# Reordering the start of a fused attention and feed-forward kernel: earlier third pair, later weight conversion, identity products

## The chip, the cores and the metric

The kernel runs on one core of a Trainium2 chip. The metric is the device time of one execution in microseconds (us), median over several executions. Engines are abbreviated as in the profile: PE is TensorE's matmuls, PEld its weight loads, DVE is VectorE, ACT ScalarE, POOL GpSimd, SP SyncE; SPq is SyncE issuing DMAs.

## The reference

Eight sequences of 448 tokens, 12 heads of 64: attention with normalised queries and keys, then a SwiGLU feed-forward layer over 3584 tokens.

```python
q_n, k_n = rmsnorm(q, g_q), rmsnorm(k, g_k)              # q, k, v: (8, 12, 448, 64) f32
scores = (1 / sqrt(64)) * q_n @ k_n^T
attn = softmax(scores); attn_out = attn @ v
x = attn_out.transpose(0, 2, 1, 3).reshape(3584, 768)
xn = rmsnorm(x, rms_g)
out = (silu(xn @ w_gate) * (xn @ w_val)) @ w_out          # 768x1536, 768x1536, 1536x768, held in f64
```

## The kernel before

The program is one hand-made schedule. It works on pairs of heads ("pair" `g`, 48 in all) and issues the steps of several pairs interleaved; the instructions of each engine stand in its stream in the order of issue. The steps of a pair (PSUM is the memory into which PE writes here, in banks):

```python
def load_pair(g):   # SP: q of both heads in one DMA, k in two
def squares(g, i):  # ACT squares q (i=0) or k (i=1); one PE step later DVE sums them,
                    # then POOL makes 1/rms and, for q, the normalised qn
def turn(g, i):     # PE transposes qn (i=0) or k (i=1); ACT (q) or DVE (k) evicts to qkT
def score(g, cs):   # PE: two key blocks for two heads = 4 products into 4 PSUM banks;
                    # ACT: 4 exponentials (row factor of k as scale)
def values(g):      # PE: exp(scores) x v
def sums(g):        # PE: denominators, "den"; DVE: reciprocal and product
```

The weights come as 64-bit floats and are converted meanwhile. One call of `convert()` is one turn of a pipeline over 72 pieces of 384 KB:

```python
def convert():                       # shortened
    n = turn_of["n"]; turn_of["n"] += 1
    # piece n-4: POOL adds the two halves
    # piece n-3: DVE joins (3 instructions)
    # piece n-2: ACT splits (2 instructions: `top`, `raw`)
    # piece n:   SP loads it (DMA `raw<-in_moe_w_...`)
    # piece n-6: SP stores the converted block (`kept<-w`)
```

The beginning, with cuts:

```python
    for g in range(2):
        load_pair(g)
    ...                                  # constants
    for g in range(2):
        load_v(g)
    ...                                  # three small loads: rg, row, row
    squares(0, 0)
    pe(idle)
    squares(0, 1)
    pe(lambda: turn(0, 1))
    convert(); convert(); bound()
    squares(1, 0); squares(1, 1)
    pe(lambda: turn(0, 0))
    convert()
    for g in range(NG + 1):
        load_pair(g + 2)
        if g <= NPAIR:
            pe(lambda: score(g, (0, 1)))
            squares(g + 2, 0); squares(g + 2, 1)
            if g == 0:
                pe(lambda: score(g, (2, 3)))
            convert()
            pe(lambda: turn(g + 1, 0)); pe(lambda: turn(g + 1, 1))
            if g:
                pe(lambda: values(g - 1))
            load_v(g + 2)
            convert()
            if g:
                pe(lambda: sums(g - 1))
                pe(lambda: score(g, (2, 3)))
            convert()
            continue
        ...
```

Of the kernel before, what the change touches and what calls it, by code (L numbers as in the profile page):

```python
# [8 lines left out]
F32 = mybir.dt.float32  # L9
# [325 lines left out]
def safe_scores(  # L335
# [20 lines left out]
    nc = tc.nc  # L356

    def pool(name, bufs, **kw):
        return ctx.enter_context(tc.tile_pool(name=name, bufs=bufs, **kw))

    NW, NH = 27, 14
    const, small = pool("c_const", 1), pool("c_small", 4)
# [5 lines left out]
    ps_s, ps_m, ps_f = pool("c_ps_s", 4, space=PSUM), pool("c_ps_m", 1, space=PSUM), pool("c_ps_f", 3, space=PSUM)  # L368
# [9 lines left out]
    def after(n, fn):  # L378
        due.append((now["t"] + n, fn))

    def pe(fn):
        now["t"] += 1
        fn()
        for item in [d for d in due if d[0] <= now["t"]]:
            due.remove(item)
            item[1]()
# [4 lines left out]
    def load_pair(g):  # L391
        if g >= NG:
            return
        b, hp = divmod(g, NPAIR)
        hs = slice(2 * hp, 2 * hp + 2)
        qk = st["qk", g] = qk_pool.tile([P, 2, 2 * NT * D], F32, name="qk")
        nc.sync.dma_start(out=qk[:, 0].rearrange("p (h n) -> p h n", h=2), in_=q[b, hs].rearrange("h (p t) d -> p h (t d)", t=NT))

        for h in range(2):
            nc.sync.dma_start(out=qk[:, 1].rearrange("p (t h d) -> p h t d", h=2, d=D)[:, h],  # L400
                              in_=k[b, 2 * hp + h].rearrange("(p t) d -> p t d", t=NT))

    def load_v(g):
        if g >= NG:
            return
        b, hp = divmod(g, NPAIR)
        vt = st["v", g] = v_pool.tile([P, 2, NT, D], F32, name="vt")
        nc.sync.dma_start(out=vt.rearrange("p h t d -> p h (t d)"),
                          in_=v[b, 2 * hp:2 * hp + 2].rearrange("h (p t) d -> p h (t d)", t=NT))
# [5 lines left out]
    def squares(g, i):  # L415

        if g >= NG:
            return
        n = 2 * NT
        if i == 0:  # L420
            st["ms", g] = small.tile([P, 2 * n], F32, name="ms")
        ms = st["ms", g]
        sq = tmp.tile([P, n * D], F32, name="sq", tag="sq", bufs=2)
        nc.scalar.activation(sq, st["qk", g][:, i], ACT.Square)  # L424

        def reduce():
            nc.vector.tensor_reduce(out=ms[:, i * n:(i + 1) * n], in_=sq.rearrange("p (n d) -> p n d", d=D), axis=AX_X, op=ALU.add)  # L427

        after(1, reduce)
        if g <= 1:  # L430

            after(1, lambda: rms_qk(g, slice(i * n, (i + 1) * n)))
            if i == 0:
                after(1, lambda: norm_q(g))
        elif i == 1:
            after(2, lambda: rms_qk(g))
            after(2, lambda: norm_q(g))
# [14 lines left out]
    def turn(g, i):  # L452

        if g >= NG:
            return
        if ("qkT", g) not in st:
            st["qkT", g] = qkT_pool.tile([128, 2, S], F32, name="qkT")
        src = st.pop(("qn", g)) if i == 0 else st["qk", g][:, 1]
        ps = (ps_m if todo else ps_f).tile([128, 512], F32, name="tr", tag="m" if todo else "f")
        for t in range(NT):  # L460
            nc.tensor.transpose(ps[:, t * P:(t + 1) * P], src[:, t * 2 * D:(t + 1) * 2 * D], ident[0:P, 0:P])  # L461
        dst, flat = st["qkT", g][:, i, :], ps[:, 0:S]
        if i == 0:
            nc.scalar.activation(dst, flat, ACT.Copy, scale=gqk[:, 0:1])  # L464
        else:
            nc.vector.tensor_copy(dst, flat)
# [28 lines left out]
    def values(g):  # L495

        vt = st["v", g]
        av = st["av", g] = ps_m.tile([128, 512], F32, name="av", tag="m")
        for c in range(NT):
            for j in range(2):  # L500
                nc.tensor.matmul(av[j * D:(j + 1) * D, 0:S], lhsT=vt[:, j, c, :], rhs=st["e", g, c, j],  # L501
                                 start=(c == 0), stop=(c == NT - 1))
# [113 lines left out]
    def room(n):  # L616
        return len(free_w) + max(len(free_h) - 4, 0) >= n
# [5 lines left out]
    def data(key):  # L623
        return st[key][0][:, 0:BW]
# [47 lines left out]
    def convert():  # L672

        n = turn_of["n"]
        if n >= TURNS or not room(1):
            return False
        turn_of["n"] += 1
        if 0 <= n - 4 < len(pieces):
            key = pieces[n - 4][0]
            st[key] = block()  # L680
            lo, top = st.pop(("cv", n - 4))
            nc.gpsimd.tensor_tensor(data(key).bitcast(I32), top, lo, ALU.add)  # L682
        if 0 <= n - 3 < len(pieces):
            st["cv", n - 3] = join(*st.pop(("cv", n - 3)))
        if 0 <= n - 2 < len(pieces):
            st["cv", n - 2] = split(st.pop(("raw", n - 2)))
        if n < len(pieces):
            st["raw", n] = load_raw(pieces[n][1])
        if 0 <= n - 6 < len(pieces):
            keep(pieces[n - 6][0])  # L690
        if turn_of["n"] == TURNS:

            free_w.extend(cv_pool.tile([128, BW], F32, name="top") for _ in range(4))
        return True
# [398 lines left out]
    ident = const.tile([128, 128], F32, name="ident")  # L1093
# [9 lines left out]
    for a in range(2):  # L1103
        rows = slice(a * D, (a + 1) * D)
        nc.scalar.dma_start(out=gq[rows, :], in_=g_q.rearrange("(p o) -> p o", o=1))
        nc.scalar.dma_start(out=gk[rows, :], in_=g_k.rearrange("(p o) -> p o", o=1))
    for g in range(2):
        load_v(g)
    rg = const.tile([128, NDC], F32, name="rg")
    nc.sync.dma_start(out=rg, in_=moe_rms_g.rearrange("(c p) -> p c", p=128))  # L1110
    row = const.tile([1, 2, D], F32, name="row")
    nc.sync.dma_start(out=row[:, 0, :], in_=g_q.rearrange("(o d) -> o d", o=1))
    nc.sync.dma_start(out=row[:, 1, :], in_=g_k.rearrange("(o d) -> o d", o=1))
    gqk = const.tile([128, 1], F32, name="gqk")

    def bound():
        nc.vector.scalar_tensor_tensor(gqk, gq, 1.0 / D**0.5, gk, ALU.mult, ALU.mult)

        nc.vector.tensor_scalar(gqk, gqk, SAFE / D, -SAFE / D, ALU.min, ALU.max)
        nc.vector.tensor_tensor(row[:, 0, :], row[:, 0, :], row[:, 1, :], ALU.mult)  # L1120
        top = const.tile([1, 1], F32, name="top")
        nc.vector.tensor_reduce(out=top, in_=row[:, 0, :], axis=AX_X, op=ALU.max, apply_absolute_value=True)
        nc.vector.tensor_scalar(flag, top, 8.0, SAFE, ALU.mult, ALU.is_gt)


    squares(0, 0)
    pe(idle)
    squares(0, 1)
    pe(lambda: turn(0, 1))
    convert()  # L1130
    convert()
    bound()
    squares(1, 0)
    squares(1, 1)
    pe(lambda: turn(0, 0))
    convert()
    for g in range(NG + 1):
        b, hp = divmod(g, NPAIR)
        load_pair(g + 2)
        if g <= NPAIR:  # L1140
            pe(lambda: score(g, (0, 1)))
            squares(g + 2, 0)
            squares(g + 2, 1)
            if g == 0:
                pe(lambda: score(g, (2, 3)))
            convert()
            pe(lambda: turn(g + 1, 0))
            pe(lambda: turn(g + 1, 1))
            if g:
                pe(lambda: values(g - 1))  # L1150
            load_v(g + 2)
            convert()
            if g:
                pe(lambda: sums(g - 1))
                pe(lambda: score(g, (2, 3)))
            convert()
            continue

        if g < NG:
# [3 lines that stand above are left out]
        if g == NPAIR + 1:  # L1163
            pe(lambda: rms_x(0))
            pe(lambda: score(g, (2, 3)))
            pe(lambda: norm_x(0))
        pe(lambda: sums(g - 1))
        if g == NPAIR + 1:
            begin(0, 15)
        elif g < NG:  # L1170
            pe(lambda: score(g, (2, 3)))
        if hp:
            fill()
            squares(g + 2, 0)
            squares(g + 2, 1)
            pe(lambda: turn(g + 1, 0))
            fill()
            pe(lambda: turn(g + 1, 1))
            fill()
            continue  # L1180
        fill(3)
        pe(lambda: turn(g + 1, 0))
        fill(1)
        pe(lambda: rms_x(b - 1))
        squares(g + 2, 0)
        squares(g + 2, 1)
        pe(lambda: turn(g + 1, 1))
        fill(len(todo))
        begin(b - 1, 16)
        pe(lambda: norm_x(b - 1))  # L1190
        fill()
# [41 lines left out]
```

## Time and profile before

| | before |
|---|---|
| time, median of 3 runs | 1632.63 us (1631.97 to 1633.83) |
| span of the profiled execution | 1629.0 us |
| PE busy | 1607.8 us |
| granted clock below full | 0.50 for 3.4 us, 20.2 to 23.6 us; the trace has no clock record before 13.4 us |
| second half of the second pair's scores starts | 30.40 us |

The last row is the landmark: PE does the same work up to it in both kernels (but for the added products), so its shift is the lead. Landmarks are read from the chain of work that ended last; a timeline has the same start 0.07 us earlier, because it lets matmuls overlap. PE is busy 99% of the span; a gain has to come from its few idle stretches or from the 3.4 us in which its clock is halved. The lines of the profile are in the prediction.

### The profile page before, as it was taken

The page shows a single profiled execution, that of the slowest core. Times are in us where ns is not written, and L with a number is a line of the kernel's source. Part 1 is how long each engine was busy: PE and PEld are TensorE (multiplying, and loading weights), DVE is VectorE, ACT ScalarE, POOL GpSimd, SP SyncE. Part 2 cuts the span into 40 slices and gives each one's busy share as a digit, 9 for nine tenths or more (in the row PEclk, how much of TensorE's full clock was granted, in tenths as well). Part 3 has the DMA queues.
Part 4 walks back from the last instruction along what each step waited for, and adds up shares of the span by engine and source line. Part 5 has one row for each costly group of instructions (what it writes and reads, how often), then busy time and mean ns, then how long its engine had stood idle before and what let it go on. Part 6 is the DMA issues. An engine that isn't in the chain of part 4 may idle for free.

```text
span 1629.0 us, 21534 instructions
## 1 busy us (share of the span) xinstructions
PE 1607.8 (99%) x7352; PEld 1136.8 (70%) x7352; DVE 871.8 (54%) x1425; ACT 499.9 (31%) x975; POOL 632.7 (39%) x569
## 2 busy tenths in 40 slices
PE   7999999999999999999999999999999999999998
PEld 3444445678855888568875788658886587969984
DVE  6988998377842545435562354624565234433431
ACT  7756563232322332233233222322332123100110
POOL 6778777344433434244333333334353322100000
PEclk9999999999999999999999999999999999999999
DMA  7756674576865555565544755466454463557651
GB/s 202 223 165 200 188 225 146 163 231 203 264 191 168 155 156 150 175 189 158 159 118 125 206 154 154 120 211 188 140 158 126 148 193 109 151 182 238 174 149 45
DMA packets 249036, 276.83 MB, mean 170 GB/s; under 512 B 66644, under 2 KB 245844, under 8 KB 248916
## 3 DMA queue, kind: packets, MB, share of 16 engines
q1 hardware_dynamic: 248596, 275.34, 56.6%
q8 instruction: 61, 1.00, 0.3%
q14 instruction: 59, 0.48, 0.1%
q10 hardware_dynamic: 320, 0.00, 0.0%
HBM read 235.93 MB, written 39.32 MB: 169 GB/s over the span
## 4 chain that ended last, share of the span: by engine, by line
PE 91%; DVE 5%; DMA 2%; ACT 1%; SPq 0%; issue 0%; POOL 0%; DVEq 0%; ACTq 0%; POOLq 0%
PE ff L797 40%; PE ff L991 21%; PE sc L476 9%; PE av L501 9%; PE den L512 3%; PE ff L892 3%; PE ff L1022 2%; PE tr L461 2%; DVE top L646 1%; DVE top L644 1%; DVE rd L520 1%; DVE top L645 1%; ACT e L480 1%; DMA qk<-in_k_dram 1%; DMA raw<-in_moe_w_out_dram 0%; DMA raw<-in_moe_w_gate_dram 0%
## 5 line engine op out<-in xcount | busy, mean ns | idle before, releaser
L797 PE MATMUL ff<-x,w 128*128 128x224 f32 x1728 | 352.3, 354 | 0.8 <-DVE u L809 0.8
L797 PEld LDWEIGHTS ff<-x,w 128*128 128x128 f32 x1728 | 324.1, 190 | 12.1 <-issue 8.6
L797 PE MATMUL ff<-xs,w 128*128 128x224 f32 x1326 | 272.5, 353 | 0.4 <-DVE cc L809 0.4
L480 ACT ACTIVATE e<-sc,rs 112x448 f32<-112x448 f32 x384 | 211.9, 635 | 192.1 <-PE sc L476 187.0
L486 POOL TENSOR_TENSOR es<-e 112x448 f32<-112x448 f32 x82 | 95.2, 1181 | 437.3 <-ACT e L480 437.3
L797 PEld LDWEIGHTS ff<-xs,w 128*128 128x128 f32 x1326 | 248.7, 190 | 5.4 <-issue 4.7
L490 POOL TENSOR_TENSOR es<-es,e 112x448 f32<-112x448 f32 x164 | 186.0, 1145 | 85.5 <-ACT e L480 79.1
L991 PE MATMUL ff<-w,h 128*128 128x384 f32 x594 | 202.8, 487 | 0.0
L520 DVE RECIPROCAL rd<-rd 128x448 f32<-128x448 f32 x41 | 121.0, 2952 | 137.6 <-ACT rd L519 137.6
L476 PE MATMUL sc<-qkT 64*112 64x448 f32 x768 | 179.0, 570 | 3.9 <-ACT qkT L464 3.9
L991 PEld LDWEIGHTS ff<-w,h 128*128 128x128 f32 x594 | 111.5, 190 | 76.6 <-issue 2.7
L501 PE MATMUL av<-e,vt 112*64 112x448 f32 x768 | 154.9, 545 | 0.0
L444 POOL TENSOR_TENSOR rs<-ms,mhalf 112x16 f32<-112x16 f32 (+1 forms) x50 | 143.7, 2875 | 4.2
L476 PEld LDWEIGHTS sc<-qkT 64*112 64x112 f32 x768 | 69.0, 174 | 97.0 <-issue 71.0
L991 PE MATMUL ff<-w,so 128*128 128x384 f32 x338 | 117.3, 488 | 1.4 <-DVE y L952 1.4
L501 PEld LDWEIGHTS av<-e,vt 112*64 112x64 f32 x768 | 50.8, 136 | 95.3 <-issue 74.5
L1022 PE MATMUL ff<-x,w 128*128 128x448 f32 x288 | 112.0, 542 | 0.0
L809 DVE TENSOR_TENSOR cc<-ff,u 128x448 f32<-128x448 f32 x84 | 52.3, 623 | 93.4 <-PE ff L797 93.0
L991 PEld LDWEIGHTS ff<-w,so 128*128 128x128 f32 x338 | 63.2, 190 | 45.9 <-DVE y L952 2.6
L427 DVE TENSOR_REDUCE ms<-sq 112x8 f32<-112x512 f32 x96 | 61.2, 677 | 52.6 <-ACT sq L424 52.6
L1022 PEld LDWEIGHTS ff<-x,w 128*128 128x128 f32 x288 | 53.3, 190 | 50.9 <-issue 49.0
L682 POOL TENSOR_TENSOR w<-top,raw 128x384 int32<-128x384 int32 x72 | 78.5, 1105 | 25.1 <-DVE top L646 7.3
(101 smaller groups left out, 1693.9 us busy)
## 6 DMA issues: line engine op xcount, KB each, us to landing
w<-kept SPq DMA_DIRECT2D x479, 192.0 KB, 3.2
w<-kept_o SPq DMA_DIRECT2D x294, 192.0 KB, 2.7
kept<-w SPq DMA_DIRECT2D x89, 192.0 KB, 3.7
top<-kept SPq DMA_DIRECT2D x73, 192.0 KB, 3.2
qk<-in_q_dram SPq DMA_DIRECT2D x48, 224.0 KB, 3.7
qk<-in_k_dram SPq DMA_DIRECT2D x96, 112.0 KB, 3.5
vt<-in_v_dram SPq DMA_DIRECT2D x48, 224.0 KB, 2.8
raw<-in_moe_w_gate_dram SPq DMA_DIRECT2D x24, 384.0 KB, 4.6
```

Source lines behind the costliest of these rows:

```text
L427: nc.vector.tensor_reduce(out=ms[:, i * n:(i + 1) * n], in_=sq.rearrange("p (n d) -> p n d", d=D), axis=AX_X, op=ALU.add)
L444: nc.gpsimd.tensor_tensor(st["rs", g][:, cols], ms, mhalf[0:P, cols], ALU.pow)
L476: nc.tensor.matmul(ps[0:P, 0:S], lhsT=qkT[r, 1, c * P:(c + 1) * P], rhs=qkT[r, 0, :], start=True, stop=True)
L480: nc.scalar.activation(e, ps[0:P, 0:S], ACT.Exp, scale=rs[:, n:n + 1])
L486: nc.gpsimd.tensor_tensor(es, st["e", g, 0, j], st["e", g, 1, j], ALU.add)
L490: nc.gpsimd.tensor_tensor(es, es, st["e", g, c, j], ALU.add)
L501: nc.tensor.matmul(av[j * D:(j + 1) * D, 0:S], lhsT=vt[:, j, c, :], rhs=st["e", g, c, j], start=(c == 0), stop=(c == NT - 1))
L520: nc.vector.reciprocal(rd, rd)
L682: nc.gpsimd.tensor_tensor(data(key).bitcast(I32), top, lo, ALU.add)
L797: nc.tensor.matmul(bank[:, w * HT:(w + 1) * HT], lhsT=wt[:, c * 128:(c + 1) * 128], rhs=x[:, c, :], start=onto is None and w == c == 0, st ...
L991: nc.tensor.matmul(ps, lhsT=a, rhs=data(("wo", b, name, c)), start=first and c == 0, stop=c == NFP - 1, skip_group_check=True)
L1022: nc.tensor.matmul(bank[w][:, 0:S], lhsT=data(key)[:, c * 128:(c + 1) * 128], rhs=st["x", 0, half][:, c, :], start=half == c == 0, stop=ha ...
```

## The change

The intent is to get PE to its steady work sooner. The third pair's load goes ahead of the second values and the weights; the third pair's squares go ahead of the first exponentials on ACT; the first weight conversions come later; the first values stand ahead of the third pair's transpositions on PE, to give its normalisation time; and 12 products of the identity with itself run on PE while it waits for data, to raise the clock. The diff, cut to its core:

```diff
-    for g in range(2):
-        load_v(g)
+    load_v(0)
+    load_pair(2)
+    load_v(1)
 ...                                  # the small loads go into load_rows(), two
 ...                                  # gain products out of bound() into gains()
+    def warm(n):
+        ps = ps_m.tile([128, 512], F32, name="warm", tag="m")
+        for _ in range(n):
+            nc.tensor.matmul(ps[:, 0:128], lhsT=ident, rhs=ident, start=True, stop=True)
     squares(0, 0)
+    warm(9)
     pe(idle)
     squares(0, 1)
     pe(lambda: turn(0, 1))
-    convert()
-    convert()
-    bound()
+    gains()
     squares(1, 0)
     squares(1, 1)
+    warm(3)
     pe(lambda: turn(0, 0))
-    convert()
+    squares(2, 0)
+    squares(2, 1)
     for g in range(NG + 1):
-        load_pair(g + 2)
+        if g:
+            load_pair(g + 3)
+        if g == 0:
+            pe(lambda: score(0, (0, 1)))
+            pe(lambda: score(0, (2, 3)))
+            for i in range(2):
+                pe(lambda: turn(1, i))
+            for _ in range(3):
+                convert()
+            load_pair(3)
+            load_v(2)
+            convert()
+            load_rows()
+            continue
         if g <= NPAIR:
             pe(lambda: score(g, (0, 1)))
 ...
+            if g == 1:
+                pe(lambda: values(0))
             pe(lambda: turn(g + 1, 0))
             pe(lambda: turn(g + 1, 1))
-            if g:
+            if g > 1:
                 pe(lambda: values(g - 1))
 ...
+            if g == 2:
+                bound()
             continue
```

More of the change, by code (lines that the diff above doesn't have):

```diff
@@ L1106, in safe_scores, with gains, load_rows, bound @@
         nc.scalar.dma_start(out=gk[rows, :], in_=g_k.rearrange("(p o) -> p o", o=1))
-    for g in range(2):
-        load_v(g)
+    load_v(0)
+    load_pair(2)
+    load_v(1)
+    gqk = const.tile([128, 1], F32, name="gqk")
     rg = const.tile([128, NDC], F32, name="rg")
-    nc.sync.dma_start(out=rg, in_=moe_rms_g.rearrange("(c p) -> p c", p=128))
     row = const.tile([1, 2, D], F32, name="row")
-    nc.sync.dma_start(out=row[:, 0, :], in_=g_q.rearrange("(o d) -> o d", o=1))
-    nc.sync.dma_start(out=row[:, 1, :], in_=g_k.rearrange("(o d) -> o d", o=1))
-    gqk = const.tile([128, 1], F32, name="gqk")
-    def bound():
+    def gains():
         nc.vector.scalar_tensor_tensor(gqk, gq, 1.0 / D**0.5, gk, ALU.mult, ALU.mult)
         nc.vector.tensor_scalar(gqk, gqk, SAFE / D, -SAFE / D, ALU.min, ALU.max)
+    def load_rows():
+        nc.sync.dma_start(out=rg, in_=moe_rms_g.rearrange("(c p) -> p c", p=128))
+        nc.sync.dma_start(out=row[:, 0, :], in_=g_q.rearrange("(o d) -> o d", o=1))
+        nc.sync.dma_start(out=row[:, 1, :], in_=g_k.rearrange("(o d) -> o d", o=1))
+    def bound():
         nc.vector.tensor_tensor(row[:, 0, :], row[:, 0, :], row[:, 1, :], ALU.mult)
@@ L1143, in safe_scores @@
             squares(g + 2, 1)
-            if g == 0:
-                pe(lambda: score(g, (2, 3)))
             convert()
+            if g == 1:
+                pe(lambda: values(0))
             pe(lambda: turn(g + 1, 0))
             pe(lambda: turn(g + 1, 1))
-            if g:
+            if g > 1:
                 pe(lambda: values(g - 1))
@@ L1152, in safe_scores @@
             convert()
-            if g:
-                pe(lambda: sums(g - 1))
-                pe(lambda: score(g, (2, 3)))
+            pe(lambda: sums(g - 1))
+            pe(lambda: score(g, (2, 3)))
             convert()
+            if g == 2:
+                bound()
             continue
```

## The prediction

> **What bounds the kernel now.** I read four views of the kernel before, in this order: the page, the waits of the tensor engine, its timeline at the beginning, and the chain of work that ended last. The page says that the tensor engine (PE) is busy throughout, at full clock.
>
> ```profile
> span 1629.0 us, 21534 instructions
> PE 1607.8 (99%) x7352; PEld 1136.8 (70%) x7352; DVE 871.8 (54%) x1425; ACT 499.9 (31%) x975; POOL 632.7 (39%) x569
> ...
> PE   7999999999999999999999999999999999999998
> ```
>
> Only the first slice (40.7 us) and the last are not full. PE idles 1629.0 - 1607.8 = 21.2 us in all, and its waits, longest first, place that idle time:
>
> ```profile
> PE tr L461 <- DMA qk<-in_k_dram: 4.9, 1, 4.9
> PE sc L476 <- ACT qkT L464: 3.9, 2, 3.2
> PE tr L461 <- POOL qn L448: 2.6, 1, 2.6
> PE ff L991 <- DVE y L952: 2.0, 3, 0.7
> ```
>
> The columns are the total, the number of times and the longest, in us. The first three, 4.9 + 3.9 + 2.6 = 11.4 us, all lie before 20 us: the first load, the first normalised queries, and the eviction of the second pair's transposed queries. The others sum to 3.6 us. The last 6 us are the final eviction and store. A change to the beginning can therefore act on those 11.4 us, and on what PE does slowly between them. The PE timeline of the beginning (start, duration) shows both:
>
> ```profile
> 4.95 0.98 PE L461 MATMUL tr<-ident,qk 112*128 112x112 f32 x4 [4.95 <-DMA qk<-in_k_dram]
> 8.52 1.01 PE L461 MATMUL tr<-ident,qn 112*128 112x112 f32 x4 [2.59 <-POOL qn L448]
> 10.26 5.54 PE L476 MATMUL sc<-qkT 64*112 64x448 f32 x16 [0.72 <-ACT qkT L464]
> ...
> 19.92 3.10 PE L476 MATMUL sc<-qkT 64*112 64x448 f32 x8 [3.21 <-ACT qkT L464]
> ```
>
> The last row, four score products, takes 3.10 us. The same four take 1.69 us in the chain at 95 us. From 20.2 to 23.6 us the granted clock is 0.50 in narrow windows: PE idled at 16.7 to 19.9 us[...]. The chain says what held it:
>
> ```profile
> 10.07 5.57 DMA qk<-in_k_dram
> 15.64 0.02 issue
> 15.66 0.04 ACTq L424
> 15.70 0.04 issue
> 15.74 0.63 ACT sq L424
> 16.37 2.10 ACT e L480 x4
> 18.47 0.44 ACT top L638
> 18.91 0.44 ACT raw L639
> 19.35 0.53 ACT qkT L464
> 19.88 0.04 issue
> 19.92 3.10 PE sc L476 x8
> 23.02 1.22 PE tr L461 x8
> 24.24 3.16 PE av L501 x16
> 27.40 3.01 PE den L512 x16
> 30.40 4.23 PE sc L476 x16
> ```
>
> ScalarE (ACT) stands in the middle: the squares of the third pair wait for its keys (the third pair's load is queued after three weight loads and landed at 15.64), the second four exponentials stand behind those squares, then a weight conversion, and only then the eviction PE needs. From 30.40 us on PE never idles for longer than 0.7 us.
>
> [...] Here they are full (DMA share 1.13 from 10 to 15 us, 311 GB/s)[...].
>
> **The change part by part.** I compare the order of instructions of both kernels engine by engine. PE has the same instructions in the same order but for 12 identity products and one move: the first values now stand before, not after, the third pair's transpositions. The landmark for the gain is the second half of the second pair's scores, 30.40 us before; everything on PE up to it is the same work in both.
>
> (1) First queries. Their path (load, squares, sums, power, product on GpSimd (POOL), ready at 8.46) is not touched: first transposition at 8.52. At full clock it ends about 0.45 us sooner; ACT evicts (0.63) and the first scores start at about 9.8 instead of 10.26.
>
> (2) Loads. The third pair takes the places of the second values, the 768-element gain load and two small rows: q at about 5.65 us, k at 6.2 and 6.8. v and the gain load issued at those times took 3.4 to 3.5 us. By then 448+448+224+448 KB = 1.6 MB have to arrive; the windows before had moved 1.46 MB by 9 us and 1.66 MB by 10 us. I estimate the last k at about 10.3 instead of 15.64.
>
> (3) ACT. New order: eviction (to 9.75), square of q (to 10.4), square of k (to 11.0), then eight exponentials without a break, 0.55 us each (2.19/4): 11.0 + 4.4 = 15.4. Their row factors are ready at 10.48 (POOL, 8.84 + 1.64). No conversion (0.88) stands before the eviction: 15.4 to 16.0. It needs the second pair's transposition: its qn on POOL comes at about 13.5, as the vector engine (DVE) no longer sits behind the row load until 10.19 before the next sums; PE is free for it at 13.7, when the fourth exponential has released a bank.
>
> (4) PE. Second scores start at 16.0 instead of 19.92: 3.9 us gained, 0.9 of it the conversion, 3.0 the squares. PE idles only some 1.5 us before them[...]. Then to the landmark: scores 1.5, values 3.16, transpositions 0.92, sums 3.01 = 8.6 us, against 30.40 - 19.92 = 10.5 before; the 1.9 difference is the half clock. The third pair's qn is ready at about 20.0 (POOL is at it from 15.9 with 3.00 + 1.04), needed at 19.2 + 1.5 = 20.7: just in time, since values come first. Landmark at about 16.0 + 8.6 = 24.6; gain 5.8 us.
>
> (5) Moved work. Four conversion turns instead of six before the loop's second round; all later turns shift by two, and two come where the earlier kernel had none, at 275 to 290 us. A turn costs DVE 0.35 + 0.36 + 0.56 = 1.27 us and ACT 0.9. From 280 to 320 us DVE is busy 15.8 of 40 us and ACT 8.6: hidden. The bound's three small operations (0.56 us) go to a later DVE gap. The identity products run while PE waits for data: nothing. I allow 0.3 us given back over the rest.
>
> Sum: 3.9 + 1.9 - 0.3 = 5.5 us; 1632.63 - 5.5 = 1627.1.
>
> **Rivals.** (a) The third pair's keys land later, the engines being full: k took 5.57 us from issue before. With that from 6.8 they land at 12.4, and everything behind slips by about 2: gain 3.5, 1629.1. For it: shares above 1.0. Against it: those 5.57 us were spent behind 1.15 MB of weights that now come after.
> (b) The clock: the identity products are too short or too early to raise it, or the gaps drop it again. Cold first scores feed the exponentials late: 0.7 us. Cold second scores and transpositions cost up to 1.9: worst, 1629.5.
> (c) DVE takes over the bound. From 101 to 280 us it is busy 164.8 of 179 us, and the chain of waits runs through conversions and weight loads for most of 126 to 232 us. If those set the pace, PE's lead would melt there: 1632. Against it: PE waits 0.4 us in all that time, and the conversions hang on PE's own steps in program order, so they move up with it; DVE has 8.6 us of 77 to spare before 101.
> (d) The two late conversions delay the reloading and subtraction of weights for the second sequence. First such product after 320 us, the subtractions begin at 288: slack of over 10 us. Nothing, or 1 us.
>
> **Range and chances.** The mechanism is on PE's path and PE bounds all that follows, so some gain is nearly sure; (a) and (b) are the likely losses and do not fully add up. A better case (all clocks full early, keys at 9.5) gives 6.5 us. Runs of one kernel spread over 1.9 us. So 1627.1, with 1625.3 to 1629.9 eight times in ten. A gain of 2% would be 32 us, more than all the idle time of PE; a loss of 2% would need a new bound for which nothing speaks: within 2% 0.985.
>
> **What would show it.** Right: the last k of the third pair before 10.5; eight exponentials in one row ending at about 15.4; second scores at 16, taking 1.5 us, with granted clock 1.00 until 25; the landmark at 24.6, and the page's PE busy time shorter by a little (half clock gone) and its idle time by about 4 us. Wrong: squares waiting on DMA beyond 11 (a); a PEclk of 0.5 at 16 to 20 or score rows of 3 us (b); new PE waits on DVE or POOL between 30 and 400 us (c, d). If the landmark comes at 24.6 but the span is shorter by under 4 us, it was given back later.

## The result, and the profile after

| | before | after |
|---|---|---|
| time, median of 6 runs each, same rounds | 1632.45 us (1631.16 to 1634.62) | 1628.20 us (1627.08 to 1629.22) |
| ratio | | 0.9972, 95% interval 0.9959 to 0.9985 |
| span of the profiled execution | 1629.0 us | 1625.3 us |
| landmark | 30.40 us | 25.08 us |

The ratio is not quite the ratio of the medians. The kernel is faster by 4.25 us in the medians and 3.7 us in the profiled executions, 0.3%, and the prediction of 1627.1 was 1.1 us under the measured median and inside its range.

The page of the changed kernel, the lines that answer to those of before and the line of the instruction queue, of which more below:

```profile
span 1625.3 us, 21571 instructions
PE 1608.9 (99%) x7376; PEld 1139.7 (70%) x7376; DVE 871.2 (54%) x1425; ACT 500.3 (31%) x975; POOL 632.2 (39%) x569
...
PE   8999999999999999999999999999999999999998
...
q8 instruction: 61, 1.00, 0.3%
```

PE's busy time went up by 1.1 us though the span fell by 3.7: the identity products are counted as busy. The timeline of PE at the beginning (start, duration, in brackets the idle time just before and what ended it):

```profile
1.35 3.75 PE L1134 MATMUL warm<-ident 128*128 128x128 f32 x18 [1.35 <-POOL ident masks.py:199]
4.97 0.57 PE L461 MATMUL tr<-ident,qk 112*128 112x112 f32 x4
5.38 0.85 PE L1134 MATMUL warm<-ident 128*128 128x128 f32 x6
8.58 0.60 PE L461 MATMUL tr<-ident,qn 112*128 112x112 f32 x4 [2.35 <-POOL qn L448]
9.91 4.45 PE L476 MATMUL sc<-qkT 64*112 64x448 f32 x16 [0.73 <-ACT qkT L464]
...
16.09 1.76 PE L476 MATMUL sc<-qkT 64*112 64x448 f32 x8 [0.81 <-DVE qkT L466]
17.78 3.23 PE L501 MATMUL av<-e,vt 112*64 112x448 f32 x16
```

The two groups of products take 3.75 + 0.85 = 4.60 us; without them PE would be busy 1604.3, 3.5 us less than before. That is the half clock gone (the granted clock is 1.00 from 4.5 us on, where its record begins): the first transpositions take 0.57 and 0.60 us instead of 0.98 and 1.01, the first scores 4.45 instead of 5.54, the second 1.76 instead of 3.10, together 3.25 us. Not all of that lies on the path, as the chain of work that ended last shows:

```profile
6.88 3.60 DMA qk<-in_k_dram
...
10.58 0.39 ACT sq L424
...
11.11 0.63 ACT e L480
...
11.78 2.58 PE sc L476 x8
14.36 0.93 PE tr L461 x8
...
15.31 0.64 DVE qkT L466
...
16.09 1.76 PE sc L476 x8
17.85 3.16 PE av L501 x16
21.00 0.92 PE tr L461 x8
21.92 3.16 PE den L512 x16
25.08 4.23 PE sc L476 x16
```

The third pair's keys land at 10.47 us (6.88 + 3.60) instead of 15.64, so ACT is done with their square before the first exponential. ACT's own rows confirm the order: eight exponentials in one stretch, then the eviction, then conversions.

```profile
10.58 0.63 ACT L424 ACTIVATE sq<-qk 112x512 f32<-112x512 f32 x1 [0.20 <-DMA qk<-in_k_dram]
11.11 4.29 ACT L480 ACTIVATE e<-sc,rs 112x448 f32<-112x448 f32 x8
15.25 0.68 ACT L464 ACTIVATE qkT<-tr,gqk 128x448 f32<-128x448 f32 x1
15.76 0.60 ACT L638 ACTIVATE top<-raw 128x384 f32<-128x384 f32 x1
```

The lead at the landmark, 30.40 - 25.08 = 5.32 us, is 3.83 us of earlier second scores (19.92 to 16.09), 1.34 of their shorter duration (3.10 to 1.76), 0.30 of shorter transpositions (1.22 to 0.92), less 0.15 of longer denominators (3.01 to 3.16).

The span is shorter by only 3.7, so about 1.5 us was given back. PE's waits (total, times, longest) say where to look:

```profile
PE tr L461 <- POOL qn L448: 2.4, 1, 2.4
PE ff L991 <- DVE y L952: 2.0, 3, 0.7
PE den L512 <- ACT e L480: 1.6, 2, 1.4
PE warm L1134 <- POOL ident masks.py:199: 1.4, 1, 1.4
PE sc L476 <- DVE qkT L466: 0.8, 1, 0.8
PE ff L797 <- DVE u L809: 0.8, 1, 0.8
```

The same wait of the denominators in the kernel before:

```profile
PE den L512 <- ACT e L480: 0.4, 1, 0.4
```

One late wait is new: before, the denominators waited 0.4 us once in all for the exponentials; now there is one wait of 1.4 us, which ends at 176.45 us. PE's row there, first of the kernel before and then of the changed kernel (the denominators of pair 9, counted from 0 as in the code: "the ninth denominators" from here on):

```profile
180.47 0.97 PE L512 MATMUL den<-es,ones 112*64 112x448 f32 x4
```

```profile
176.45 0.97 PE L512 MATMUL den<-es,ones 112*64 112x448 f32 x4 [1.41 <-ACT e L480]
```

Up to 125 us the denominators of the two kernels start 5.3 us apart; here they are 180.47 - 176.45 = 4.02 apart, and 3.8 at the end of the attention part. Nothing else changed: from 182 to 600 us PE idles 1.54 us before and 1.40 after. ACT's rows just before it show why the exponentials were late:

```profile
172.52 0.58 ACT L638 ACTIVATE top<-raw 128x384 f32<-128x384 f32 x1 [2.51 <-DMA raw<-in_moe_w_val_dram]
173.00 0.55 ACT L639 ACTIVATE raw<-raw 128x384 int32<-128x384 uint32 x1
174.79 0.56 ACT L638 ACTIVATE top<-raw 128x384 f32<-128x384 f32 x1 [1.23 <-DMA raw<-in_moe_w_gate_dram]
175.25 0.54 ACT L639 ACTIVATE raw<-raw 128x384 int32<-128x384 uint32 x1
175.69 2.18 ACT L480 ACTIVATE e<-sc,rs 112x448 f32<-112x448 f32 x4
```

A split of a weight piece stands in ACT's queue ahead of the exponentials and waits 1.23 us for the piece, although the scores had been there since about 172. And SyncE's issue of that very load is odd:

```profile
168.01 0.37 SPq L629 DMA_DIRECT2D raw<-in_moe_w_val_dram  x1
168.44 0.48 SPq L670 DMA_DIRECT2D kept<-w  x1
169.01 1.99 SPq L629 DMA_DIRECT2D raw<-in_moe_w_gate_dram  x1
171.05 0.48 SPq L670 DMA_DIRECT2D kept<-w  x1
```

It takes 1.99 us where an issue of the same form takes 0.37, and the piece lands 5.70 us after it was begun, at 174.71. At the same moment, at 168.9 us, a packet of the queue that the profile calls "instruction" begins. The DMA view of 168.6 to 170.6 us (packets, MB, share of 16 engines):

```profile
q1 hardware_dynamic: 261, 0.27, 60.8%
q8 instruction: 1, 0.02, 5.8%
```

There are 61 such packets in this queue, q8, in the execution, of 16,384 bytes each and about 1.1 us long on average. I counted that between two of them PE starts mostly 220 to 290 matmuls and weight loads, so I take them for fetches of PE's instructions: an estimate from this count, which no view of the profile shows as such. ("Fetch" below is always a packet of q8; there is a second, smaller instruction queue, q14, told of with the tiny loads.) In the kernel before, the sixth fetch comes at 186.0 us, after the ninth denominators, and the loads in front of them were all issued in about 0.4 us.

### The profile page after: what moved, and what is told of

Same layout as the page of the kernel before. It is cut to its first block, busy times and chain, and to the rows that moved or that the text cites. A ratio compares the mean times of both kernels' runs of the same rounds, so it can differ in the third digit from the quotient of the medians.

```text
span 1625.3 us, 21571 instructions
## 1 busy us (share of the span) xinstructions
PE 1608.9 (99%) x7376; PEld 1139.7 (70%) x7376; DVE 871.2 (54%) x1425; ACT 500.3 (31%) x975; POOL 632.2 (39%) x569
## 4 chain that ended last, share of the span: by engine, by line
PE 91%; DVE 5%; DMA 2%; ACT 1%; issue 0%; POOL 0%; SPq 0%; DVEq 0%; ACTq 0%; POOLq 0%
PE ff L797 41%; PE ff L991 21%; PE sc L476 9%; PE av L501 9%; PE den L512 3%; PE ff L892 3%; PE ff L1022 2%; PE tr L461 2%; DVE top L646 1%; DVE top L645 1%; DVE rd L520 1%; DVE top L644 1%; DMA raw<-in_moe_w_out_dram 0%; ACT e L480 0%; PE rb L558 0%; DMA raw<-in_moe_w_val_dram 0%
## 5 line engine op out<-in xcount | busy, mean ns | idle before, releaser
L797 PE MATMUL ff<-x,w 128*128 128x224 f32 x1770 | 359.3, 353 | 0.8 <-DVE u L809 0.8
L797 PEld LDWEIGHTS ff<-x,w 128*128 128x128 f32 x1770 | 332.2, 190 | 9.8 <-issue 6.7
L1022 PEld LDWEIGHTS ff<-x,w 128*128 128x128 f32 x288 | 53.3, 190 | 50.9 <-issue 49.0
## 6 DMA issues: line engine op xcount, KB each, us to landing
w<-kept SPq DMA_DIRECT2D x480, 192.0 KB, 3.2
w<-kept_o SPq DMA_DIRECT2D x290, 192.0 KB, 2.8
kept<-w SPq DMA_DIRECT2D x94, 192.0 KB, 3.7
top<-kept SPq DMA_DIRECT2D x72, 192.0 KB, 3.0
```

The lines of the kernel that those rows point to most:

```text
L797: nc.tensor.matmul(bank[:, w * HT:(w + 1) * HT], lhsT=wt[:, c * 128:(c + 1) * 128], rhs=x[:, c, :], start=onto is None and w == c == 0, st ...
L1022: nc.tensor.matmul(bank[w][:, 0:S], lhsT=data(key)[:, c * 128:(c + 1) * 128], rhs=st["x", 0, half][:, c, :], start=half == c == 0, stop=ha ...
```

## The experiments

Three theories for the 1.5 us given back were tested, besides the parts of the gain:
- F: a fetch of PE's instructions coincides with a weight load's issue and delays it, and the 12 products shifted the fetch there.
- L: the lead melts whatever the products are, because conversions set the pace around 126 to 232 us (the prediction's rival (c)); the loss should grow with the lead.
- S (an early form of F): the fetch belongs to SyncE's own stream, so more DMA issues move it.

All kernels gave correct results; four to six runs each. All figures are together here. "Lead" is 30.40 minus the landmark; "lead at 9th" is 180.47 minus the start of the ninth denominators; "wait" is PE's wait for ACT just before them; "fetch" is the sixth packet of the instruction queue; "slow issue" is the issue of the last weight piece that ACT converts ahead of the exponentials in question, or of the one before it, where it took over 1.1 us. The columns from the landmark on come from one profiled execution of each kernel.

| kernel | median us (range) | ratio to before [95%] | landmark | lead → lead at 9th | wait | fetch | slow issue |
|---|---|---|---|---|---|---|---|
| changed kernel | 1628.20 (1627.08 to 1629.22) | 0.9972 [0.9959, 0.9985] | 25.08 | 5.32 → 4.02 | 1.41 | 168.9 | 1.99 |
| again | 1628.06 (1627.61 to 1630.02) | 0.998 [0.9963, 0.9996] | 25.91 | 4.49 → 3.66 | 0.86 | 169.3 | 1.96 |
| no_products | 1627.26 (1626.57 to 1627.79) | 0.997 [0.9953, 0.9987] | 26.61 | 3.79 → 3.57 | none | 182.6 | none |
| values_late | 1629.14 (1627.96 to 1630.12) | 0.9982 [0.9965, 0.9999] | 27.32 | 3.08 → 2.43 | 0.76 | 170.8 | 2.19 |
| weights_first | 1632.13 (1631.24 to 1632.72) | 1.0002 [0.9985, 1.0019] | 29.75 | 0.65 → -0.24 | 1.02 | 173.0 | 1.19 |
| extra3 | 1627.65 (1626.74 to 1628.04) | 0.9977 [0.996, 0.9994] | 25.78 | 4.62 → 3.73 | 1.01 | 169.1 | 2.38 |
| extra8 | 1627.56 (1626.21 to 1628.90) | 0.998 [0.9964, 0.9997] | 24.97 | 5.43 → 4.69 | 0.85 | 168.3 | 2.05 |
| before_extra14 | 1638.78 (1636.97 to 1640.22) | 1.0049 [1.0033, 1.0066] | 31.25 | -0.85 → -6.24 | none | 192.0 | none |
| products_alone | 1633.63 (1632.45 to 1634.48) | 1.0017 [1.0, 1.0033] | 28.71 | 1.69 → -0.60 | 2.37 | 172.5 | 1.11 |
| narrow_alone | 1632.54 (1630.53 to 1635.35) | 1.001 [0.9994, 1.0026] | 28.93 | 1.47 → 0.17 | 1.34 | 172.4 | 1.27 |
| narrow_products | 1628.09 (1627.55 to 1629.68) | 0.998 [0.9964, 0.9995] | 26.57 | 3.83 → 3.04 | 0.93 | 170.1 | 2.36 |
| more_products | 1627.39 (1627.23 to 1629.14) | 0.9976 [0.9962, 0.9989] | 25.24 | 5.16 → 3.65 | 1.59 | 168.5 | 1.17 |
| wide_products | 1627.17 (1626.22 to 1627.77) | 0.9969 [0.9955, 0.9982] | 25.87 | 4.53 → 4.76 | none | 178.5 | none |

The stretch alone, without the lead: from the start of pair 8's denominators to that of pair 9's PE takes 28.87 to 29.21 us in the four traces whose fetch lies elsewhere (before, no_products, before_extra14, wide_products), and 29.80 to 31.41 us in the ten where it stands beside the load. In these ten the slow issue ends 0.14 to 0.42 us after the fetch's packet does, whether the packet took 0.96 us or 2.10.

### The changed kernel once more

No edit; it says how far two runs of one program differ.

> The changed kernel once more, unaltered, to see what repeats. Landmark = start of the second half of the second pair's scores: 25.1 us in the changed kernel's trace, 30.4 in the earlier one's. My theory of the lost part: at 169.0 us the SyncE queue stands 2 us at one weight load because its own instruction stream is being fetched just then (a 16 KB instruction packet starts at 168.9), the load lands 1.6 us late, ScalarE's exponentials stand behind its conversion, and PE waits 1.4 us for them at 175. The fetch comes at a fixed place of the stream, so the wait must be there again, 1.2 to 1.6 us. Rival: a chance delay of the DMA engines; then the wait is gone or elsewhere, and the span is about 1624. Rival two: the conversion chain on VectorE sets the pace; then the wait is there too.

Landmark 25.91, 0.83 later than in the first profile. The clock did it: here it was half for one stretch of 3.41 us, from 10.93 to 14.34 us, so that the first scores took 5.27 us instead of 4.45; the first profile of the same program has no such stretch there. The loss by the ninth denominators is there again (0.83 us, with a wait of 0.86 where 1.2 to 1.6 was expected), and so is the slow issue (1.96 us at 169.41, beside a fetch at 169.3).

### The identity products taken out

```diff
-    warm(9)
...
-    warm(3)
```

> The changed kernel without the 12 identity products. Theory: without them PE is at half clock[...], so the first scores feed the exponentials late: landmark 0.7 us later than in the run of the unaltered kernel (25.8), second scores still at full clock (1.8 us). Rival: the products are what keeps the second scores warm too; then these take 3 us and the landmark is past 27. Rival two: they are worth nothing, 25.1.

The row of the second scores in PE's timeline:

```profile
17.62 1.76 PE L476 MATMUL sc<-qkT 64*112 64x448 f32 x8 [0.87 <-ACT qkT L464]
```

They start 1.53 us later than in the first profile of the changed kernel and 0.70 later than in its second; they take 1.76 us, so the clock is full by then without any product (from 15.08 us on). By the landmark the products are worth 0.70 us against the second profile of the changed kernel, which had the half clock from 10.93 to 14.34 us, and 1.53 us against the first, whose record shows full clock from 4.5 us to past the landmark. But the kernel is not slower: 1627.26, and its ratio of 0.997 is beside the 0.998 of the changed kernel in the same rounds. The ninth denominators do not wait; the fetch is at 182.6 us. What the products win at the beginning, the wait at 176 us takes back. This fits F; L could still say that a smaller lead loses less.

### The first values back behind the third pair's transpositions

```diff
-            if g == 1:
-                pe(lambda: values(0))
             pe(lambda: turn(g + 1, 0))
             pe(lambda: turn(g + 1, 1))
-            if g > 1:
-                pe(lambda: values(g - 1))
+            pe(lambda: values(g - 1))
```

> The changed kernel with one move undone: the first values again behind the third pair's transpositions. Theory: PE then asks for the third pair's normalised queries at 17.9 us, and GpSimd has them at 20.1: PE idles 2.2 us, landmark 27.3, span 2.2 us longer than the unaltered kernel's. Rival: the queries are no bound; landmark 25.1.

```profile
20.17 0.60 PE L461 MATMUL tr<-ident,qn 112*128 112x112 f32 x4 [1.49 <-POOL qn L448]
```

The transposition has to wait 1.49 us for POOL's normalised queries. The landmark is 27.32, against 25.91 in the repeat, which had as slow first scores (5.27 us, here 5.24): the move is worth 1.4 us there. In the time it shows as about 1 us (1629.14 against 1628.06), with ranges that overlap.

### Two conversion turns back ahead of the third pair's load

```diff
     load_v(0)
+    convert()
+    convert()
     load_pair(2)
     load_v(1)
...
-            for _ in range(3):
+            for _ in range(1):
                 convert()
```

> The changed kernel with only the order of SyncE's loads altered: two weight loads (768 KB) stand ahead of the third pair's load again; every compute engine has the unaltered order. Theory: the DMA engines are full, 768 KB at about 300 GB/s delay the third pair's last keys by 2.6 us (10.5 to 13.1), the eight exponentials begin 2.6 us later, landmark 27.7. Rival: the keys' landing is hidden behind other work of ScalarE; landmark below 25.6.

ACT's timeline:

```profile
12.58 0.63 ACT L424 ACTIVATE sq<-qk 112x512 f32<-112x512 f32 x1 [2.83 <-DMA qk<-in_q_dram]
13.88 0.63 ACT L424 ACTIVATE sq<-qk 112x512 f32<-112x512 f32 x1 [0.67 <-DMA qk<-in_k_dram]
14.41 3.24 ACT L480 ACTIVATE e<-sc,rs 112x448 f32<-112x448 f32 x6
```

With two weight loads in front the third pair's keys land 3.3 us later (13.78 against 10.47; 2.6 was expected), the exponentials start 3.3 us later, PE idles (2.07 us between the two halves of the first scores), and the clock is at half from 9.34 to 12.76 and from 16.17 to 19.58 us. The landmark is 29.75 where 27.7 was expected; the lead is 0.65 us and the time that of the kernel before, 1632.13 against 1631.52. So the order of these loads is what all the rest of the gain depends on; putting the squares ahead of the exponentials without it wins nothing. And against L: with almost no lead to lose, the kernel still lost 0.89 us by the ninth denominators, with the fetch at 173.0 beside an issue of 1.19 us.

### Small loads added, to move SyncE's stream

Tiny loads on SyncE's queue, 16 bytes each, into a tile that nobody reads; 3 and 8 in the changed kernel, 14 in the kernel before, all at the third pair:

```diff
+    def extra():
+        for i in range(n):
+            nc.sync.dma_start(out=spare[:, i, :], in_=g_q[0:4].rearrange("(o d) -> o d", o=1))
...
             if g == 2:
                 bound()              # absent in the kernel before
+                extra()
```

> The changed kernel with three tiny loads (16 bytes each, never read) put into SyncE's stream at about 45 us; every other engine is unaltered. In five traces of the changed order the sixth 16 KB fetch of SyncE's stream falls on the 137th DMA issue, a weight load that the exponentials wait for; the three loads should move it three issues earlier, to the 134th of the old numbering, a store followed by 8 idle us of SyncE. Theory: the denominators' waits for exponentials, 1.5 us in all, fall to 0.5 or less, and PE keeps its gain: 1.0 us shorter than the unaltered kernel's run. Rival (the conversion chain on VectorE sets the pace): waits stay 1.5 us.

> The same with eight tiny loads: the fetch should fall eight issues earlier, on the 129th of the old numbering, also a weight load, but one issued at the start of a longer pause. Theory: no wait at the denominators of 176 us (0.5 us or less in sum), perhaps a smaller one before. Rival (the tiny loads themselves help or harm, or the DVE sets the pace): the same as with three, or 1.5 us.

> The kernel before with fourteen tiny loads in SyncE's stream at about 50 us. Its sixth fetch falls behind the 151st issue, into a pause; fourteen loads should bring it to the 137th or 138th, between the weight loads at 174 us. Theory: the kernel that had no wait there gets one: the denominators' waits for exponentials grow from 0.4 to about 1.5 us, and it is 1 us slower from there on. Rival (the wait comes from the new order of the conversions): 0.4 us as before.

The expectation on the fetch failed in all three, and theory S with it: with 3 and 8 more issues ahead, the fetch still fell on the same weight load (169.1 and 168.3 us), and the 14 in the kernel before did not bring it forward (192.0; that kernel was late by then, and PE had started as many instructions at its fetch, 1478, as in the kernel before, 1477). From here on I took the fetches for PE's. What the tiny loads did move are packets of the second instruction queue, q14 (8,192 bytes each, 59 in the execution): one came at 173.5 us with 8 loads instead of 178.3, and with 14 at 174.5 instead of 183.1. That SyncE's own stream is in that queue is my estimate from these two shifts; no slow weight load stands beside these packets. The third run did something else: it was 0.5% slower. In PE's waits:

```profile
PE sc L476 <- ACT qkT L464: 4.8, 2, 4.0
PE tr L461 <- POOL qn L448: 4.6, 2, 2.6
```

The second line had one wait in the kernel before, now two, the new one of 2.0 us at 61 us: the tiny loads stood in front of a pair's queries and keys in the queue. About 4.6 us of lead were gone there, part of it with the clock at half once more just after this idle time (62.3 to 65.8 us): the values there took 4.92 us, where they take 3.23 at full clock.

### The products alone, in the kernel before

```diff
     squares(0, 0)
+    warm(9)
     pe(idle)
...
     squares(1, 1)
+    warm(3)
     pe(lambda: turn(0, 0))
```

The second of these kernels has the same 12 products with one column each (`ps[:, 0:1]`, `rhs=ident[:, 0:1]`).

> The kernel before with the 12 identity products alone. Theory: the third pair's keys still land at 15.6 us and ScalarE still has squares, exponentials and a conversion before the eviction, so the second scores start at 19.9 as before; landmark 30.4, at best 29.5[...]. Time within 1 us of before but for what a shifted instruction fetch adds. Rival: the clock is the main part of the gain; landmark below 28.

> The kernel before with 12 products of one column in place of the 12 identity products: the same number of PE instructions, next to no work. The tiny loads showed that the 16 KB fetches are not of SyncE's stream: they stayed where they were. New theory: they are PE's ([...]PE and its weight loads have 15,095 to 15,137), so 12 more products move them against the loads. Expected: landmark at 30.4 us as before or up to 1.7 less, the fetch near 172 to 175 us instead of 186.0, and the denominators' waits for exponentials at 1.3 us or more instead of 0.4. Rival (the identity products' early lead is what brings the wait): with the landmark at 30.4 the waits stay 0.4.

Neither helps: 1633.63 and 1632.54 against 1631.52 and 1632.05. At the landmark they lead by 1.69 and 1.47 us, because no half-clock stretch fell on the second scores (1.76 us in both, not 3.10). Those scores start at 19.80 and 20.01, as before: the products do not touch what PE waits for. By the ninth denominators this lead is gone, with waits of 2.37 and 1.34 us; the fetch is at 172.5 and 172.4 us instead of 186.0, as narrow_alone's expectation had it (172 to 175 us, wait 1.3 or more). These two are the strongest case against L: the order of all other work is that of the kernel before, which waits nothing there, and 12 products bring the wait; in products_alone the loss, 2.29 us, is larger than the lead there was to melt. The conversion schedule is two turns ahead in this order, so that another piece is hit than in the changed kernel. SyncE's row in the first of them

```profile
172.73 1.11 SPq L629 DMA_DIRECT2D raw<-in_moe_w_val_dram  x1
```

and of the same piece in the kernel before:

```profile
174.46 0.38 SPq L629 DMA_DIRECT2D raw<-in_moe_w_val_dram  x1
```

ACT gets this piece only at 179.43 us, 6.7 us after the issue began; in the kernel before it is split from 178.76, after 4.3 us. The issue alone (0.7 us longer) explains less than half of that: the transfer was longer too.

### Products with one column, and more products, in the changed kernel

```diff
-            nc.tensor.matmul(ps[:, 0:128], lhsT=ident, rhs=ident, start=True, stop=True)
+            nc.tensor.matmul(ps[:, 0:1], lhsT=ident, rhs=ident[:, 0:1], start=True, stop=True)
```

```diff
-    warm(3)
+    warm(7)
```

> The changed kernel with one column in place of 128 in its 12 products. Theory: as in the kernel without them the clock comes up only with the scores (landmark 26.0 to 26.7), but with the fetch back at 169 to 171 us the denominators' waits are 1.0 us or more, where the kernel without them had 0.5; span about 1 us longer than that one's. Rival: no wait, span as without them.

> The changed kernel with seven instead of three products in the second group. They fit into the idle time before the first queries where the clock is full by then (5.4 to 7.4 us, queries at 8.6). Two effects expected: [...]the clock falls less often (landmark 25.1 to 25.5), and PE's fetch moves 16 to 32 instructions, 3 to 6 us, ahead, to 163 to 166 us, where SyncE issues nothing: denominators' waits 0.6 us or less in sum, span 1624.3. Rival: the waits stay at 1.5 us wherever the fetch is; span 1625.5 or more. If the products at half clock are too long, the first scores come late and the landmark is 26 or more.

The narrow products keep PE's instruction count and take away its columns. The landmark (26.57) is that of no products at all (26.61): they do not raise the clock, which is full only from 13.95 us, although PE's records of them are no shorter (4.00 + 1.30 us) than those of the products of 128 columns (3.75 + 0.85), with which it is full from 4.5 us. The fetch stays beside the load (170.1 us, issue 2.36), and 0.79 us of the lead is lost, where no_products with the same landmark lost 0.22. So in these runs the fetch went with the number of PE's instructions, not with their length: 168.9 us with twelve products of 128 columns, 170.1 with twelve of one column, 182.6 with none.

Four more products were meant to bring the fetch ahead of the load. They did not: 168.5 us, issue 1.17, wait 1.59. That part of the expectation failed. The clock stayed full from 5.47 us on and the landmark is as good as in the first profile.

### The same columns in fewer instructions

```diff
-            nc.tensor.matmul(ps[:, 0:128], lhsT=ident, rhs=ident, start=True, stop=True)
+            nc.tensor.matmul(ps[:, 0:384], lhsT=ident,
+                             rhs=ident.unsqueeze(1).to_broadcast([128, 3, 128]), start=True, stop=True)
...
-    warm(9)
+    warm(3)
...
-    warm(3)
+    warm(1)
```

> The changed kernel with the same number of columns of identity products, but as three products of 384 columns and one of 384 instead of nine and three of 128: a third of PE's instructions for them, so the sixth 16 KB fetch of PE's instructions should come a few us later than in the changed kernel (I work it out as about 178 us: 64 instructions fewer of the 96, between 169 us with all and 182.6 with none), clear of the 137th issue of SyncE at about 169 us. Theory that the fetch slows that weight load: its issue takes about 0.4 us, the wait of the denominators at 176 us for the exponentials is at most 0.6 us (changed kernel 1.4), and of the lead at the landmark (25.0 to 26.0 us) at most 0.8 us is lost by the end; time 0.7 to 1 us under the changed kernel, about 1626.8. Rival theory, that the loss comes from having the products at all or from the lead itself: the wait is again 0.9 us or more, and the lead lost 1.0 to 1.7, time about 1628. If the fetch does not move off the issue, the run tells nothing on it.

This was the one test with a lead of 4 to 5 us and the fetch elsewhere. The fetch came at 178.5 us, as hoped. SyncE's rows:

```profile
169.35 0.38 SPq L629 DMA_DIRECT2D raw<-in_moe_w_gate_dram  x1
169.78 0.61 SPq L670 DMA_DIRECT2D kept<-w  x1
```

PE's row of the ninth denominators, and the wait for the exponentials in the whole execution:

```profile
175.71 0.95 PE L512 MATMUL den<-es,ones 112*64 112x448 f32 x4
```

```profile
PE den L512 <- ACT e L480: 0.3, 1, 0.3
```

The issue takes 0.38 us instead of 1.99, the piece lands after 4.56 us instead of 5.70, PE doesn't wait, and no lead is lost: 4.53 at the landmark, 4.76 at the ninth denominators, 4.51 at the end of the attention part (3.81 in the changed kernel). L expected 0.9 us of wait or more. F stands. The kernel still has both warm() calls, and each of them takes a tile of the pool `ps_m`, so that a shifted order of PSUM buffers is not what brings the wait. In the time the difference is at the edge of what can be seen: 1627.17 here (ratio 0.9969), the changed kernel 1628.20 (0.9972), in different rounds with overlapping intervals. The profiled span is 1624.4, which it shares with extra8 as the shortest of all. It is the version I would keep, but no run shows it to beat the changed kernel beyond the spread.

The working by which I placed the fetch at 178 is not borne out as a rule: it took the shift as proportional to the added instructions, and four more products moved nothing. I counted PE's instructions other than products up to the sixth fetch: 1480 with no products, 1465 with the 16 added matmuls and weight loads of the wide ones, and 1385 and 1383 with 48 and 64. What fixes the steps stays open.

How general the coincidence is, I counted in five traces (before, after, again, no_products, wide_products): of 71 DMA issues of over 1.1 us, 56 begin within 0.5 us of one of the packets of q8, while only 239 of all 7055 issues do, 3.4%. All of these 56 end 0.14 to 0.45 us after the packet does, about the 0.37 us of a usual issue; that such an issue begins its work only then is my estimate from these times, and no trace shows it as such. The smaller packets of q14 are a control: 2 of the 71 slow issues begin within 0.5 us of one, and 216 of all 7055. Not every issue that meets a packet is slow: in all 14 traces 573 begin during a packet of q8, and 251 of these end before it does.

## Why the prediction was right

**First queries (1).** Right. First transposition at 8.58 (predicted 8.52, 0.4 shorter as said), first scores at 9.91 (9.8).

**Loads (2).** Right: last keys of the third pair at 10.47 (10.3, and "before 10.5"). weights_first shows that the whole gain hangs on this: keys at 13.78, and nothing is left. Rival (a), keys at 12.4 and a gain of 3.5, did not come; weights_first is that rival made on purpose, and it cost more than (a) supposed; there the clock was also at half from 9.34 to 12.76 and from 16.17 to 19.58 us.

**ACT (3).** Right: eight exponentials without a break, ending at 15.40 (15.4), and the eviction at 15.93 (16.0). The keys' eviction on DVE ended at about the same moment, so the wait is entered under DVE; it makes no difference.

**PE (4).** Right in its mechanism, small in two terms: second scores at 16.09 (16.0), taking 1.76 instead of the 1.5 that was reckoned (the prediction's own line at 95 us has 1.69), and denominators 3.16 instead of 3.01. The landmark is 25.08 instead of 24.6, a lead of 5.32 instead of 5.8. The move of the first values was needed as argued: normalised queries at 20.06 (20.0), and 1.49 us of wait without it. What the prediction treated as fixed, the half clock on the second scores, does not come in every trace: the products-alone kernels start them at about the same time (19.80 and 20.01 us, before 19.92) and have them at full clock (1.76 us). Of the four traces of the old order two have it (before and before_extra14, 3.10 and 2.77 us) and two have not (1.76). So the 1.9 us that the prediction put down to the clock, measured 1.64 (1.34 in the scores and 0.30 in the transpositions), are in part luck of the one execution that was profiled; how often the other executions had the half clock there is not shown.

**The clock, rival (b).** It happened in part in the repeat: cold first scores (5.27 us instead of 4.45), 0.83 us at the landmark, about as (b) had put it (0.7).

**Moved work (5).** This is the step that failed. "The identity products run while PE waits for data: nothing. I allow 0.3 us given back over the rest." The products do run in idle time, but with them the sixth fetch comes at 168.9 us, without them at 182.6, and at 168.9 it lies on the issue of a weight load whose conversion stands ahead of exponentials on ACT: 1.3 us lost by the ninth denominators and 1.5 by the end instead of 0.3; in wide_products, with the fetch elsewhere, nothing is lost by the ninth denominators. The rest of step (5) held: the waits in the feed-forward part are equal in both kernels (2.0, 0.8 and 0.4 us), so the two late conversion turns cost nothing that shows.

**Rival (c).** It named the right stretch, 126 to 232 us, and half the mechanism: the chain through weight load and conversion is that tight there. But DVE was not the bound and the lead did not melt: it is lost in one wait, also where there is hardly a lead (weights_first), and not where there is one and the fetch is elsewhere (wide_products). **Rival (d)** did not come.

**The sum.** Predicted 3.9 + 1.9 - 0.3 = 5.5; in the profiles 5.3 - 1.5 = 3.8 (the spans differ by 3.7); in the medians 4.25. Of the 1.7 us between 5.5 and the profiles' 3.8, 1.2 is the sum's last term and 0.5 the short durations at the landmark. The sign that PE's busy time would fall was wrong as written, since the added products are counted in it.

Left open: whether and by what the fetch holds the issue, and why only some issues; whether and how it lengthens the transfer beyond that (2.4 us in products_alone, of which the issue is 0.7; the wait does not grow with the issue: 1.59 us with an issue of 1.17, 1.01 with one of 2.38); and what fixes the fetch's place to the instruction.

## What to carry to other kernels

Look for what stands in an engine's queue in front of the instruction that the bound engine needs: here the gain hung on moving one load forward and two squares ahead (second scores at 16.09 us instead of 19.92), and it was lost when the load went back (20.76). Keep the landmark in both traces and subtract: where the lead shrinks, there is one wait to be explained. Instructions put into idle time were not free here: with twelve products the sixth fetch came at 168.9 us instead of 182.6, beside the issue of a load with no slack (1.99 us instead of 0.37), and PE's wait of 1.41 us cost about what the products had won by the landmark, 0.7 to 1.5 us; four longer products, with the fetch at 178.5 us, came without this wait.
